# Alternating the products of two Strassen–Winograd multiplications on two PSUM banks each, with sums asked for earlier and half of k-by-v one step later

## The chip, the cores and the metric

The kernel runs on one core of one Trainium2 chip. The metric is the device time of one execution in microseconds (us). Before the change it took 991.92 us in the median of three runs (988.21 to 992.99).

Names in the profile: PE is TensorE's matmul, PEld its weight load, DVE is VectorE, ACT is ScalarE, POOL is GpSimd, SP issues DMAs. "L86" is a line of the kernel; here it is a helper through which every matmul goes (L87 in the changed kernel), as L400 (L405) is for adds, so rows are told apart by the names of their tiles.

## The reference

```python
# q, k, v: 8 batches x 8 heads x 576 x 64, float32;  g_norm: 64
kv  = einsum('bhsd,bhse->bhde', k, v)
out = einsum('bhsd,bhde->bhse', q, kv)
rms = sqrt(mean(out * out, axis=-1, keepdims=True) + 1e-6)
x   = (out / rms * g_norm)            # -> 4608 x 512 (tokens x heads*dim)
h   = x @ w_in                        # 512 -> 2048
g   = maximum(0.01 * h, h)
y   = g @ w_out                       # 2048 -> 512; result 4608 x 512
```

The weights reach the kernel as 64-bit floats and are rounded to 32 bits on the chip, in 32 pieces.

## The kernel before

The 4608 rows are nine blocks of 512. The first block is multiplied in the plain way while weights still arrive and are rounded (`first_block`; tiles `h_ps`, `o_acc`). The other eight use Strassen–Winograd, a scheme that multiplies two matrices, each cut into 2x2 blocks, with seven products of sums of blocks instead of eight, for x·w_in ("h") and for g·w_out ("o"), in four chunks of the hidden width per block. One product is four matmuls of 256 columns (8 entries in the trace, f32). Most products are added to an earlier one in a PSUM bank (a piece of the memory that TensorE writes its results to), and after each of them some engine reads the bank.

```python
BANK = {1: "a", 6: "a", 7: "a", 4: "a", 2: "b", 5: "c", 3: "c"}

def strassen(which, left, right, done):
    banks = {}
    for i in (1, 5, 2, 6, 3, 7, 4):
        first = BANK[i] not in banks
        if first:
            banks[BANK[i]] = ps_m.tile([P, 2, N2], F32, tag=f"{which}{BANK[i]}", ...)
        bank = banks[BANK[i]]
        ...                        # four matmuls into bank
        done(i, bank)              # the reader: an add on VectorE or a copy / leaky relu on ScalarE
        yield

# main loop, per block i and chunk c   (h of chunk c; o of the chunk before)
x_sides = sides_x(xTs.pop(i))      # sums of x, VectorE
...
first = product_h(c, x_sides, g_sides)   # asks for the sums of w_in (GpSimd) itself
go(first, 1)                       # h1
go(second)                         # what is left of the older o
for n in range(5):                 # h5 h2 h6 h3 h7
    go(first, 1)
    if n in (1, 3): go(a_steps, 1) # one step of the attention of a later batch
second = product_o(*before) if before else iter(())
go(second, 1)                      # o1
go(first)                          # h4
for n in range(5):                 # o5 o2 o6 o3 o7
    go(second, 1)
    if n in (1, 3): go(a_steps, 1)
```

The attention steps of a batch, and their places in the first block:

```python
def attention(b):
    ...
    for p in range(NP):            # four pairs of heads
        nc.vector.transpose(qT[:, p, :]..., q_in...)        # 1.25 us on VectorE
        if p % 2 == 0: yield; continue
        attention_kv(b, p // 2, kv_ps)                      # k by v, TensorE, 72 entries
        ...                        # loads of the next two pairs are issued here
        yield
    copy_kv(b, kv_ps); yield       # VectorE
    ...                            # q by kv into o_ps, squares, sums, division

steps.update((i, a1) for a1 in [attention(1)]
             for i in (12, 13, 16, 17, 19, 21, 23, 24, 25, 27, 28))   # first block
```

Rounding one piece of weights takes two ScalarE copies (`add`, `cut`) and four VectorE steps. The 64-bit data lie in one of seven buffers in turn; four of them (`pair0` to `pair3`) later hold GpSimd's sums of weights:

```python
raw_homes = itertools.cycle([(stage, "raw")] * 3 + [(wcomb, f"pair{i}") for i in range(4)])

def round_f64(dst, raw):
    add = spare(...); nc.scalar.activation(add, lo, func=AF.Copy, scale=2.0 ** -29)
    cut = spare(...); nc.scalar.activation(cut, hi..., func=AF.Copy, scale=2.0 ** -112)
    nc.vector.tensor_scalar(cut, cut, ...)               # 1
    nc.vector.tensor_scalar(dst, cut, 3, ...)            # 2
    nc.vector.scalar_tensor_tensor(dst, cut, ..., dst)   # 3
    nc.vector.tensor_tensor(dst, dst, add, op=ALU.add)   # 4
```

## Time and profile before

| | before |
|---|---|
| median of three runs | 991.92 us |
| span of the profiled run | 990.2 us |
| TensorE busy | 958.0 us (97%) |
| TensorE waits from 150 us on | 16.6 us |

At 97% the number that matters is not the busy share but the list of the holes on TensorE. There are two ways to read one. The view of waits gives the idle time with the engine and tile that ended it. The timeline gives more: start to start, an undisturbed product takes 1.73 us here, so whatever exceeds that is lost, whether it was waiting, refilling or a slower clock. The prediction shows both.

For the comparison I cut a span at two points that every variant has: the start of the `o_acc` group just ahead of the attention output of 448 columns in the first block (E, 103.50 us here), and the first Strassen product `h_a` (151.19). The piece between them is F, 47.7 us, the end of the first block; the rest is S, 839.0 us, the eight Strassen blocks.

### The profile page before, as it was taken

What the parts mean: (1) busy time and instruction counts of PE and PEld (TensorE: products, weight loads), DVE (VectorE), ACT (ScalarE), POOL (GpSimd) and SP (SyncE); (2) the same over time, 40 slices, a digit from 0 to 9 for tenths busy, and PEclk for the clock granted to TensorE, in tenths of its full rate; (3) what the DMA queues carried; (4) which work ended last, traced back from release to release, by engine and by line L of the source; (5) the groups of instructions that cost most, each with busy time, mean ns of one, the idle gap of its engine ahead of it and who ended that gap; (6) DMA issues with size and microseconds to landing.
All of it is one profiled execution on the core that took longest, in us unless ns stands there. A gap on an engine that the chain in (4) does not pass through costs nothing.

```text
span 990.2 us, 14098 instructions
## 1 busy us (share of the span) xinstructions
PE 958.0 (97%) x5702; PEld 763.8 (77%) x5702; DVE 435.3 (44%) x688; ACT 268.1 (27%) x531; POOL 499.0 (50%) x395
## 2 busy tenths in 40 slices
PE   8899987999999999999999999999999999999997
PEld 4444435878887888888887888788878888888885
DVE  3968971264234533364335433552245322422223
ACT  3645432331124211421133113311242112112210
POOL 1000214455655665566556666565556666666642
PEclk9899999999999999999999999999999999999999
DMA  9989505300260008000610043003100010001001
GB/s 251 243 214 239 164 1 138 96 1 1 56 178 1 1 2 231 2 1 1 178 56 1 1 121 113 1 1 96 45 1 1 1 43 1 1 1 43 1 1 42
DMA packets 36160, 63.47 MB, mean 64 GB/s; under 512 B 4864, under 2 KB 21248, under 8 KB 36096
## 3 DMA queue, kind: packets, MB, share of 16 engines
q1 hardware_dynamic: 26112, 51.95, 19.9%
q10 hardware_dynamic: 9856, 10.62, 3.2%
q8 instruction: 45, 0.74, 0.3%
q14 instruction: 19, 0.16, 0.1%
q0 software_dynamic: 128, 0.00, 0.0%
HBM read 53.12 MB, written 9.44 MB: 63 GB/s over the span
## 4 chain that ended last, share of the span: by engine, by line
PE 90%; DVE 6%; DMA 2%; ACT 1%; issue 1%; SPq 0%; ACTq 0%; DVEq 0%
PE h_a L86 22%; PE o_a L86 21%; PE h_c L86 11%; PE o_c L86 11%; PE h_b L86 6%; PE o_b L86 6%; PE o_acc L86 5%; PE h_ps L86 5%; PE kv_ps L86 2%; PE o_ps L86 2%; DVE qT L327 1%; DVE sum L289 1%; DMA k_in<-in_k_dram 1%; DMA v_in<-in_v_dram 1%; DMA raw<-in_moe_w_in_dram 1%
## 5 line engine op out<-in xcount | busy, mean ns | idle before, releaser
L400 DVE TENSOR_TENSOR o<-o_a,o 128x512 f32<-128x512 f32 x104 | 71.5, 688 | 122.2 <-PE o_a L86 122.2
L86 PE MATMUL o_a<-wt,gs 128*128 128x256 f32 x512 | 122.1, 381 | 0.0
L400 POOL TENSOR_TENSOR ws<-w 128x512 f32<-128x512 f32 x32 | 44.3, 1385 | 136.6 <-PE h_a L86 97.1
L400 POOL TENSOR_TENSOR wt<-w,w 128x512 f32<-128x512 f32 x32 | 40.9, 1277 | 140.5 <-PE o_a L86 137.4
L86 PEld LDWEIGHTS o_a<-wt,gs 128*128 128x128 f32 x512 | 96.3, 190 | 15.2 <-issue 2.1
L479 ACT ACTIVATE g<-g 128x512 f32<-128x512 f32 x96 | 60.5, 630 | 167.4 <-DVE g L400 167.4
L400 POOL TENSOR_TENSOR gs<-g,g 128x512 f32<-128x512 f32 x64 | 81.3, 1270 | 23.0 <-ACT g L479 22.5
L400 POOL TENSOR_TENSOR ws<-w,w 128x512 f32<-128x512 f32 x32 | 41.9, 1310 | 97.4 <-DMA raw<-in_moe_w_in_dram 94.6
L484 ACT COPY g<-h_a 128x512 f32<-128x512 f32 x32 | 18.7, 585 | 255.5 <-PE h_a L86 244.4
L400 POOL TENSOR_TENSOR wt<-w,wt 128x512 f32<-128x512 f32 x64 | 83.4, 1303 | 2.5
L400 POOL TENSOR_TENSOR wt<-w 128x512 f32<-128x512 f32 x32 | 41.2, 1289 | 65.6 <-PE o_a L86 60.0
L86 PE MATMUL h_a<-xt,w 128*128 128x256 f32 x256 | 62.6, 388 | 7.8 <-DVE g L400 7.8
L86 PE MATMUL h_ps<-xT,w 128*128 128x512 f32 (+1 forms) x136 | 60.5, 589 | 8.1 <-DVE xT L308 4.8
L400 DVE TENSOR_TENSOR g<-h_b,g 128x512 f32<-128x512 f32 x32 | 22.1, 689 | 98.0 <-PE h_b L86 98.0
L400 DVE TENSOR_TENSOR o<-o_c,o 128x512 f32<-128x512 f32 x56 | 38.4, 685 | 57.6 <-PE o_c L86 57.6
L86 PE MATMUL o_a<-wt,g 128*128 128x256 f32 x256 | 60.8, 380 | 1.9 <-DVE o L400 1.9
L86 PE MATMUL h_a<-xT,ws 128*128 128x256 f32 x256 | 62.4, 386 | 0.0
L86 PEld LDWEIGHTS h_a<-xt,w 128*128 128x128 f32 x256 | 48.8, 193 | 17.2 <-DVE g L400 10.6
L86 PE MATMUL h_a<-xT,w 128*128 128x256 f32 x256 | 62.0, 386 | 0.0
L86 PE MATMUL o_a<-w,g 128*128 128x256 f32 x256 | 60.6, 379 | 0.8 <-DVE o L400 0.8
L86 PE MATMUL h_a<-xt,ws 128*128 128x256 f32 x256 | 61.1, 382 | 0.0
L86 PE MATMUL o_c<-wt,gs 128*128 128x256 f32 x256 | 60.8, 381 | 0.0
(86 smaller groups left out, 1741.1 us busy)
## 6 DMA issues: line engine op xcount, KB each, us to landing
out_dram<-o ACTq DMA_DIRECT2D x36, 256.0 KB, 2.2
v_in<-in_v_dram SPq DMA_DIRECT2D x30, 288.0 KB, 5.0
raw<-in_moe_w_in_dram SPq DMA_DIRECT2D x64, 128.0 KB, 5.5
raw<-in_moe_w_out_dram SPq DMA_DIRECT2D x16, 512.0 KB, 6.2
k_in<-in_k_dram SPq DMA_DIRECT2D x28, 288.0 KB, 3.5
q_in<-in_q_dram SPq DMA_DIRECT2D x56, 144.0 KB, 4.5
q_in<-in_q_dram SPq DMA_DIRECT2D x56, 140.0 KB, 4.6
k_in<-in_k_dram ACTq DMA_DIRECT2D x2, 288.0 KB, 9.2
```

Source lines behind the costliest of these rows:

```text
L86: pin(nc.tensor.matmul(*args, **kw))
L289: nc.vector.tensor_add(sums[l], sums[l], sq)
L327: nc.vector.transpose(qT[:, p, :].rearrange("p (t s) -> p s t", s=T), q_in.rearrange("p (s d) -> p s d", d=D)[:, :, :32])
L400: eng.tensor_tensor(out_, a, b_, op=ALU.subtract if minus else ALU.add)
L479: nc.scalar.activation(t, t if src is None else src, func=AF.Prelu, alpha=SLOPE)
L484: nc.scalar.copy(g11, bank)
```

## The change

Its intent: no product should have to wait for the reader of the bank that it writes, and a load should not be waited for. So h and o alternate strictly, the order of the seven products is chosen so that two banks each suffice and alternate too, the second half of k by v comes one step later, and sums are asked for ahead. The core of the diff:

```diff
-        for p in range(NP):
-            ...transpose of pair p...
-            if p % 2 == 0:
+        for m in range(2):
+            turn(2 * m)
+            yield
+            turn(2 * m + 1)
+            if m:
                 yield
-                continue
-            attention_kv(b, p // 2, kv_ps)
+            attention_kv(b, m, kv_ps)
 ...
     def sides_w1(c):                     # sides_w2 likewise
 ...
-        return {1: a11, 2: a12, 3: s4, 4: a22, 5: s1, 6: s2, 7: s3}
+        def more():                      # sums for products 7 and 3, asked for later
+            ...
+        return sides, more
 ...
-    BANK = {1: "a", 6: "a", 7: "a", 4: "a", 2: "b", 5: "c", 3: "c"}
+    ORDER = (1, 2, 6, 5, 7, 3, 4)
+    FRESH = (1, 2, 5)
 ...
+            b = "a" if i in (1, 6, 7, 4) else "c"
 ...
-        accs = [... for t in ("ha", "hb", "oa", "ob")]
+        accs = [... for t in ("oa", "oc", "hb", "ob")]
 ...
-                 for i in (12, 13, 16, 17, 19, 21, 23, 24, 25, 27, 28))
+                 for i in (12, 13, 15, 16, 18, 20, 21, 23, 24, 26, 27, 28))
 ...
+            for t in range(7):
+                go(h_steps, 1)
+                go(o_steps, 1)
+                if t == 3:
+                    h_next, more_h = sides_w1((c + 1) % NC)
+                    o_next, more_o = sides_w2(c)
+                if t == 5:
+                    more_h()
+                if (7 * c + t) % 2:
+                    go(a_steps, 1)
+                if c == NC - 1 and t == 4 and i + 1 < NB:
+                    go(a_steps)
+                    x_sides, more_x = sides_x(xTs.pop(i + 1))
```

## The prediction

> **What bounds the kernel now.** I read the page first: part 1 says who is busy, part 4 who is on the path.
>
> ```profile
> PE 958.0 (97%) x5702; PEld 763.8 (77%) x5702; DVE 435.3 (44%) x688; ACT 268.1 (27%) x531; POOL 499.0 (50%) x395
> ...
> PE 90%; DVE 6%; DMA 2%; ACT 1%; issue 1%; SPq 0%; ACTq 0%; DVEq 0%
> ```
>
> TensorE works for 97% of the span, so a mere change of order can win only the holes between its matmuls and the stretches at a lower clock. The change adds no matmul: the two built kernels have 542 rows each on TensorE, in another order. So I list the holes. The view of waits, TensorE only, from 150 us on (the Strassen part):
>
> ```profile
> PE h_a L86 <- DVE g L400: 7.8, 7, 2.1
> PE kv_ps L86 <- DMA v_in<-in_v_dram: 6.1, 2, 5.1
> PE o_a L86 <- DVE o L400: 2.7, 4, 0.9
> ```
>
> The waits sum to 16.6 us. They cost more than that, so I price them from start to start. In the timeline of TensorE an undisturbed product (4 matmuls of 256 columns, 8 entries) starts 1.73 us after the one before. Around the worst hole:
>
> ```profile
> 161.13 2.00 PE L86 MATMUL h_a<-xT,ws 128*128 128x256 f32 x8
> 163.90 1.99 PE L86 MATMUL h_a<-xt,w 128*128 128x256 f32 x8 [0.78 <-DVE g L400]
> 166.96 0.29 PE L86 MATMUL kv_ps<-v_in,k_in 64*64 64x64 f32 x2 [1.06 <-DMA v_in<-in_v_dram]
> 172.31 2.19 PE L86 MATMUL kv_ps<-v_in,k_in 64*64 64x64 f32 x70 [5.06 <-DMA v_in<-in_v_dram]
> 174.43 3.45 PE L86 MATMUL h_a<-xT,w 128*128 128x256 f32 x8
> 177.72 1.89 PE L86 MATMUL h_c<-xt,ws 128*128 128x256 f32 x8
> ```
>
> From 163.90 to 177.72 lie 13.82 us for two products and one k-by-v group (1.21 us start to start elsewhere): 1.73+1.73+1.21 = 4.67. **Loss 9.15 us**, of which 6.1 is waiting; the rest is the slow clock after it (3.29 us for the product at 174.43). The next kind, again TensorE alone:
>
> ```profile
> 425.09 1.89 PE L86 MATMUL o_a<-w,g 128*128 128x256 f32 x8
> 427.93 1.99 PE L86 MATMUL h_a<-xt,w 128*128 128x256 f32 x8 [0.95 <-DVE g L400]
> ```
>
> 2.84 instead of 1.73. Two products of h into bank a stand with one product between; the reader of the bank, an add on VectorE, stood behind attention work. This happens at 321, 425, 530, 634 and 738 us (1.1 each; with two small ones, 0.45 in sum: 6.1). Its bad case is at 217.91 (wait 2.12, then 3.15 and 2.10 us for two products): 4.1. The tail has three more, where bank a follows bank a directly: 967.07 to 969.84 to 972.59, and 981.32 to 984.09, 1.04 each: 3.1. **Sum of holes after 163 us: 9.15+6.1+4.1+3.1 = 22.4 us.**
>
> **What the Trainium skill says.** "TensorE: Matmul & The Clock Gate", The HAM clock gate: after an idle window of about 3.4 us the array runs at half clock until it has been busy again for as long. The trace agrees in the factor (3.29 against 1.73) but a wait of 2.12 us was already enough at 217.91, while waits of 1.5 us and less left the clock alone. "SBUF — State Buffer", Who interferes with whom: VectorE and GpSimd share one port pair, an exclusive lock; two-input adds and 2-port modes on VectorE block against a reading GpSimd. The trace agrees: the rounding of weights, VectorE, with GpSimd idle (first three rows) and with GpSimd adding from 138.98 to 143.56 (last three):
>
> ```profile
> 137.15 0.43 DVE L197 TENSOR_SCALAR w<-cut 128x512 uint32<-128x512 uint32 x1
> 137.61 0.69 DVE L198 SCALAR_TENSOR_TENSOR w<-cut,w 128x512 uint32<-128x512 uint32 x1
> 138.33 0.69 DVE L200 CUSTOM_DVE_ANT_0 w<-w,add 128x1024 uint16<-128x1024 uint16 x1
> ...
> 139.40 1.37 DVE L197 TENSOR_SCALAR w<-cut 128x512 uint32<-128x512 uint32 x1
> 140.80 1.63 DVE L198 SCALAR_TENSOR_TENSOR w<-cut,w 128x512 uint32<-128x512 uint32 x1
> 142.47 1.64 DVE L200 CUSTOM_DVE_ANT_0 w<-w,add 128x1024 uint16<-128x1024 uint16 x1
> ```
>
> "PSUM — Partial Sum Buffer", PSUM bank collisions: the bank must be guarded as a whole. That is why a product waits for its bank's reader even if it accumulates.
>
> **The change part by part.**
>
> 1. *Interleave, two banks each.* The built order is h1 o1 h2 o2 h6 o6 h5 o5 h7 o7 h3 o3 h4 o4, banks a c a c a c a for each of h and o (o1 is of the chunk before). Between two uses of a bank there are now three products (5.2 us), except that h4 and the next h1, and o4 and the next o1, have one. A reader starts some 0.2 us after its product's next has started and takes 0.6 (ScalarE) to 0.69 us (VectorE), so with one product between it has 0.75 us to spare, with three over 4. The h4 reader is a ScalarE activation now, and on VectorE the order near o4 has no attention instruction next to it. I went through the heaviest stretch (last chunk of a block: two qT transposes of 1.26, sums, the division): the tightest add there has about 1.5 us left. So the five 1.1 us waits and the 4.1 us event go: **-10.2 us**. In the first chunk, which has no o to put between, h4 to h1 is adjacent, about 1.0 us; it replaces the 1.04 at 161.13. Net 0.
> 2. *Second k-by-v group later.* In the built order it stands nine products after the first, not one. Its loads are issued when the first group ends (161.2 us) and the last landed at 172.3: 11.1 us, against 9 x 1.73 = 15.6 us of room. The wait and its slow clock go: **-9.15 us**.
> 3. *Tail.* The last o alternates a and c; only o4 to o1 is adjacent. Two of three waits go: **-2.1 us**.
> 4. *Sums moved.* GpSimd has 12 adds of 1.27 us per chunk of 14 products: 15.2 of 24.2 us, as before. Sums of weights come half a chunk ahead, since each pair buffer is refilled as soon as its second product is read. In the last chunk it makes four sums of weights that nobody uses (401 rows against 397), 5 us beside the matmuls. Sums of x: same adds, two steps ahead. **0 us.**
> 5. *End of the first block.* Here the order of two engines changes. Now TensorE loses 1.3 and 1.7 us:
>
> ```profile
> 134.34 3.60 PE L86 MATMUL o_acc<-w,gT 128*128 128x512 f32 x8
> 139.08 3.70 PE L86 MATMUL h_ps<-xT,w 128*128 128x512 f32 x8 [1.15 <-DVE w L200]
> 144.25 7.11 PE L86 MATMUL o_acc<-w,gT 128*128 128x512 f32 x16 [1.47 <-DVE w L200]
> ```
>
> Two of the three last weight pieces are rounded earlier in the new order, so these 3.0 us go. But the very last piece (the weights of the last o_acc group) now stands on ScalarE behind the activation of the last h_ps, and the same event lets GpSimd start its sums. Counting from 134.34: the last h_ps ends at 134.34+2x3.43 = 141.2; activation and two ScalarE copies about 1.9, so 143.1; four VectorE steps at the blocked durations 0.42+1.37+1.63+1.64 with gaps 5.2, so 148.4. The last o_acc could have started at 141.2+3.43 = 144.7. New wait 3.7, and after so long a wait I expect the half clock, some 2 us more (1.8 at 217.91, 3.0 at 172). **-3.0+5.7 = +2.7 us.**
>
> Sum: 990.2-10.2-9.15-2.1+2.7 = 971.5 us of span; the timed run is 1.7 longer than its span (991.89 against 990.2): 973.2. I add 0.8 for small new waits (a 512-wide attention output on ScalarE just ahead of an h4 reader, an issue of a store behind an add): **974.0 us**, 1.8% less.
>
> **The rivals.**
>
> *A: VectorE becomes the bound between products.* For: 44% busy in bursts, and its reads of o are now interleaved with h. Against: 3 products between uses of a bank, and 10 adds of 0.69 are only 6.9 of 24.2 us per chunk. If the one-product places (two per chunk, 62 in all) each lost 0.3 us, +19 us: about 990, nothing won.
>
> *B: GpSimd.* Its sums of g, w and the weights stand in one queue. For: 63% load in the Strassen part and refills that wait for a product to be read. Against: from the end of h3 the six sums and two refills take about 9 us, and the first user, o6, comes 8 products (13.8 us) after h3. If wrong, each chunk could lose some us: 1000 and more.
>
> *C: the loads were the only gain.* If the small waits come back elsewhere, only part 2 and the tail are won: 990.2-11.2+2.7+1.7 = 983.
>
> *D: the end of the first block goes well* (last piece rounded without the block, or the clock kept): 2 to 4 us less: 970 to 972, just over 2%.
>
> **Range and chances.** The holes bound the gain: 22.4 us after 163 and 3.0 in the first block, so nothing under 966 is possible, and 2% means under 972.1 (against the median 991.92; the three runs before spread over 4.8 us). My sum ends 2 us above that line, with part 5 (2.7) the least sure; what I overlooked is likelier a new wait than a new gain. Range 969 to 982; faster by over 2%: 0.25, within 2%: 0.73, slower: 0.02.
>
> **What would show it.** TensorE's waits after 150 us should fall from 16.6 to about 2 to 4 us, with no DMA wait on kv_ps; the waits on "g" for h_a gone or turned into one on ScalarE's activation in the first chunk. In the tail one wait instead of three. About 148 us a wait of 3 to 4 us of o_acc for a rounded weight, followed by a product or two at half clock; if it is missing, part 5 is wrong and the time is near 970. Per-product pitch stays at 1.73. Many waits of h_a on ScalarE or o_a on VectorE at the seams of chunks would make A right; waits on ws, wt or gs of GpSimd, B.

## The result

| | before | after |
|---|---|---|
| median, same chip, 4 runs each | 992.45 us (988.21 to 993.62) | 977.11 us (976.25 to 978.28) |
| span of the profiled run | 990.2 us | 974.5 us |
| E / F / S | 103.5 / 47.7 / 839.0 | 103.4 / 54.1 / 817.0 |

The ratio is 0.9854, with a 95% interval of 0.9827 to 0.9881: 1.5% less time, inside the 2% band. Ratios are the mean time of one kernel's runs over that of the other's runs of the same rounds, so they are not quite the ratio of the medians quoted.

From the page of the kernel after, part 1 and the engines' shares of the chain that ended last (the prediction shows these for the kernel before):

```profile
PE 954.6 (98%) x5702; PEld 762.3 (78%) x5702; DVE 430.2 (44%) x688; ACT 270.1 (28%) x531; POOL 507.9 (52%) x399
...
PE 94%; DVE 2%; DMA 2%; ACT 1%; issue 0%; SPq 0%; ACTq 0%
```

The matmuls are as many as before. VectorE's share of the chain fell from 6% to 2%. The waits of TensorE from 150 us on, after (total us, times, longest):

```profile
PE o_acc L87 <- DVE w L201: 3.7, 1, 3.7
PE o_a L87 <- DVE o L405: 0.8, 1, 0.8
PE h_a L87 <- ACT g L484: 0.7, 1, 0.7
```

That is 5.2 us instead of 16.6, and of these 3.7 belong to the first block. The wait for `v_in` is gone. Busy time in the stretch from 160 to 200 us; columns: stretch, its length, PE, PEld, DVE, ACT, POOL busy with counts, granted clock, DMA share, GB/s. First before:

```profile
160.00:200.00 40.00, 33.10 (x294) 26.92 (x295) 11.02 (x18) 11.75 (x23) 21.22 (x17) 0.91 0.47 118
```

Then after:

```profile
160.00:200.00 40.00, 39.31 (x325) 33.15 (x324) 9.13 (x13) 11.68 (x22) 22.36 (x18) 1.00 0.46 119
```

TensorE is busy for 39.3 of 40 us instead of 33.1, and the granted clock is 1.00 instead of 0.91: both the wait for the load and the slow clock behind it are gone. From 200 to 900 us it is busy all the time, in every hundred.

So the Strassen part gained 22.0 us, and the end of the first block gave 6.4 back. Where? The timeline of TensorE in the first block, before:

```profile
103.50 3.60 PE L86 MATMUL o_acc<-w,gT 128*128 128x512 f32 x8
107.02 0.98 PE L86 MATMUL o_ps<-qT,kv 64*32 64x448 f32 x16
107.94 3.70 PE L86 MATMUL h_ps<-xT,w 128*128 128x512 f32 x8
```

And after:

```profile
103.44 3.60 PE L87 MATMUL o_acc<-w,gT 128*128 128x512 f32 x8
108.62 1.16 PE L87 MATMUL o_ps<-qT,kv 64*32 64x448 f32 x12 [1.58 <-DVE kv L260]
...
110.84 3.70 PE L87 MATMUL h_ps<-xT,w 128*128 128x512 f32 x8
```

From the first row to the last it is 4.44 us before and 7.40 after: 2.96 us lost. The copy of kv comes at 108.30 on VectorE instead of 103.73. k by v itself, at 95.26 instead of 91.89, had long ended by then, and both kernels round 25 weight pieces ahead of the copy. What is new is a wait of VectorE for a ScalarE copy (`cut`), whose queue now holds an activation ahead of it. ScalarE and then VectorE, after:

```profile
95.37 0.60 ACT L565 ACTIVATE gT<-h_ps 128x512 f32<-128x512 f32 x1 [5.16 <-PE h_ps L87]
```

```profile
97.13 0.43 DVE L195 TENSOR_SCALAR cut<-cut 128x512 f32<-128x512 f32 x1 [4.55 <-ACT cut L194]
```

In the kernel before, the ScalarE copies of five pieces ran from 89.05 to 94.92 us with no activation between them, and VectorE shows no idle time from 90.31 until the copy of kv. Now only the first of these pieces comes ahead of the activation, which waits for `h_ps` until 95.37. VectorE's 4.55 us of idle time match the 4.57 by which the copy is late. The end of the block, after:

```profile
151.36 6.32 PE L87 MATMUL o_acc<-w,gT 128*128 128x512 f32 x8 [3.65 <-DVE w L201]
157.51 1.89 PE L87 MATMUL h_a<-xT,w 128*128 128x256 f32 x8
```

The last `o_acc` group waits 3.65 us for the last rounded weight piece, and then takes 6.15 us start to start instead of 3.51 (the same group at full clock, in the run "GpSimd's sums wait for the last piece" below): 2.64 us for the half clock. The granted clock is 0.50 from 149.9 to 156.7 us (view of windows in steps of 0.2 us). VectorE's last three rounding steps, which it waits for, after:

```profile
146.50 1.37 DVE L198 TENSOR_SCALAR w<-cut 128x512 uint32<-128x512 uint32 x1
147.91 1.63 DVE L199 SCALAR_TENSOR_TENSOR w<-cut,w 128x512 uint32<-128x512 uint32 x1
149.57 1.64 DVE L201 CUSTOM_DVE_ANT_0 w<-w,add 128x1024 uint16<-128x1024 uint16 x1
```

And GpSimd at the same time, in the same run:

```profile
146.09 1.51 POOL L405 TENSOR_TENSOR ws<-w 128x512 f32<-128x512 f32 x1 [26.80 <-ACT cut L194]
```

GpSimd had idled for 26.8 us and was released by the same ScalarE copy (`cut`) as VectorE, because the raw data of that last piece lay in the buffer (`pair0`) that its sums fill.

### The profile page after: what moved, and what is told of

It reads as the page before. It is cut to its first block, busy times and chain, and to the rows that moved or that the text cites. A ratio compares the mean times of both kernels' runs of the same rounds, so it can differ in the third digit from the quotient of the medians.

```text
span 974.5 us, 14053 instructions
## 1 busy us (share of the span) xinstructions
PE 954.6 (98%) x5702; PEld 762.3 (78%) x5702; DVE 430.2 (44%) x688; ACT 270.1 (28%) x531; POOL 507.9 (52%) x399
## 4 chain that ended last, share of the span: by engine, by line
PE 94%; DVE 2%; DMA 2%; ACT 1%; issue 0%; SPq 0%; ACTq 0%
PE h_a L87 23%; PE o_a L87 23%; PE h_c L87 17%; PE o_c L87 17%; PE h_ps L87 5%; PE o_acc L87 5%; PE o_ps L87 2%; DMA k_in<-in_k_dram 2%; PE kv_ps L87 2%; DMA raw<-in_moe_w_in_dram 1%; DVE w L199 0%; DVE w L201 0%; ACT cut L194 0%; DVE qT L329 0%; DVE xT L309 0%
## 5 line engine op out<-in xcount | busy, mean ns | idle before, releaser
L405 POOL TENSOR_TENSOR ws<-w 128x512 f32<-128x512 f32 x33 | 46.4, 1407 | 288.6 <-PE h_c L87 247.7
L405 DVE TENSOR_TENSOR o<-o_c,o 128x512 f32<-128x512 f32 x88 | 60.5, 687 | 89.5 <-PE o_c L87 89.5
L405 DVE TENSOR_TENSOR g<-h_c,g 128x512 f32<-128x512 f32 x64 | 44.0, 688 | 85.6 <-PE h_c L87 85.6
L87 PE MATMUL o_acc<-w,gT 128*128 128x512 f32 x128 | 60.7, 619 | 3.7 <-DVE w L201 3.7
L87 PE MATMUL h_c<-xT,w 128*128 128x256 f32 x256 | 61.1, 381 | 0.0
L87 PE MATMUL h_c<-xt,ws 128*128 128x256 f32 x256 | 61.1, 381 | 0.0
L87 PE MATMUL h_c<-xT,ws 128*128 128x256 f32 x256 | 60.5, 379 | 0.0
```

Of the source, the lines that this page charges most:

```text
L87: pin(nc.tensor.matmul(*args, **kw))
L405: eng.tensor_tensor(out_, a, b_, op=ALU.subtract if minus else ALU.add)
```

## The experiments

Ten kernels ran, three rounds each; a ratio is to the runs of the kernel before on the same chip (medians 992.45 to 993.37). All outputs are right. E, F and S are those of each profiled run. Against the line of 2% only the last two of the table are faster; the first block in the old order is unclear, since its interval holds 0.98.

| run | median us | ratio to before (95%) | E | F | S |
|---|---|---|---|---|---|
| before | 992.45 | 1 | 103.5 | 47.7 | 839.0 |
| after | 977.11 | 0.9854 (0.9827, 0.9881) | 103.4 | 54.1 | 817.0 |
| k by v later alone | 981.47 | 0.9881 (0.9866, 0.9895) | 105.5 | 47.7 | 826.6 |
| all but k by v later | 982.50 | 0.9892 (0.9877, 0.9906) | 104.8 | 53.1 | 821.2 |
| three banks, old order | 979.97 | 0.9866 (0.9849, 0.9884) | 105.6 | 54.5 | 819.3 |
| sums not ahead | 977.38 | 0.9841 (0.9824, 0.9858) | 104.5 | 54.3 | 817.2 |
| two reads more at o4 | 996.06 | 1.0035 (1.0018, 1.0053) | 104.5 | 53.1 | 835.9 |
| two reads more at o2 | 977.65 | 0.9845 (0.9830, 0.9859) | 104.2 | 54.3 | 817.7 |
| last piece elsewhere | 977.99 | 0.9849 (0.9834, 0.9863) | 104.0 | 55.8 | 816.7 |
| first block in the old order | 973.34 | 0.9804 (0.9787, 0.9820) | 106.2 | 47.7 | 817.1 |
| sums wait for the last piece | 971.90 | 0.9784 (0.9768, 0.9799) | 104.9 | 48.6 | 817.0 |
| both of the last two | 969.85 | 0.9765 (0.9751, 0.9780) | 105.6 | 46.0 | 817.0 |

The theory after the result: the alternation wins what bank readers cost, the distance between the halves of k by v wins the load wait, and the first block gives 6.4 us back for two reasons: kv's copy is late (2.96), because ScalarE's copies for the rounding are, and VectorE and GpSimd block each other at the last piece (3.4 net of what the reorder won). The rivals: the later k by v is the whole gain; the number of banks or VectorE's load is what matters; the losses in the first block have another cause.

### k by v later alone

The kernel before with the new attention steps for batches 2 and on, nothing else.

```diff
-        a_steps = attention(i + 1) if i + 1 < B else iter(())
+        a_steps = attention_new(i + 1) if i + 1 < B else iter(())   # second half one step later
```

> The kernel before, with nothing changed but the second k-by-v group one step later in batches 2 to 7. In the built order five products stand between the two groups in block 1 instead of two. Theory (the wait at 167 to 172 us is the time of the loads, 11.1 us after the first group): 5 x 1.73 + 1.0 of room leave a wait of about 1.5 us and no half clock, so 7 to 8 us less than before, about 984.5 us; the 1.1 us waits of h_a on VectorE's adds at five places and the tail's three waits stay. Rival (the loads come later by as much as the group is moved): no gain, 992.

Measured: 981.47 us, 3 us better than expected. No wait for the load is left (I had expected 1.5 us), and S fell by 12.4 us, more than the 9.15 of the load wait. The excess is the bad event at 217.91 us (4.1 us in the prediction): with the attention steps shifted by one, the wait there is 0.59 us and the clock stays up. The small VectorE waits did not go; they changed their tile. TensorE's waits for VectorE's add into o in this run:

```profile
PE o_a L86 <- DVE o L427: 6.6, 9, 0.9
```

Before there were seven waits on g (7.8 us) and four on o (2.7); now there is one on g and nine on o. The add that happens to stand behind attention instructions on VectorE makes its bank late: at 425 us in the kernel before the add into g (427.21, after two transposes), in this run the one into o (425.74, after two transposes).

### All but k by v later

The changed kernel with the old attention steps for batches 2 and on.

```diff
-        a_steps = attention(i + 1) if i + 1 < B else iter(())
+        a_steps = attention_old(i + 1) if i + 1 < B else iter(())   # second half as before
```

> The changed kernel with the second k-by-v group at its old step in batches 2 to 7 (the first block as in the changed kernel). In the built order five products (8.7 us, with 0.7 of wait 9.4) stand between the groups of batch 2, eight (13.8 us) in later batches, against loads of about 11 us. Theory (the interleave alone has already moved the groups apart): one wait of 1.5 to 2 us for v in block 1, with at most 2 us of half clock after it, none later: 979 to 981 us. Rival (the later group is what removed the 9.15 us): a wait of 5 us as before, 985 or more.

Measured: 982.50 us, outside what I had expected. And the expected wait for v is not there. TensorE in this run:

```profile
175.90 1.28 PE L87 MATMUL kv_ps<-v_in,k_in 64*64 64x64 f32 x72
...
228.82 1.99 PE L87 MATMUL o_a<-w,g 128*128 128x256 f32 x8 [1.46 <-DVE o L428]
```

The second half of k by v starts at 175.90 us, 11.0 us after the first half (164.90), without a wait: the new loop spaces the attention steps two turns apart, and that is enough for the load. What this run lost is at 228.82 and, with waits of 0.95 and 0.30 us, at two other seams: o1 waits for the add of o4, which at 228 us stood on VectorE behind two transposes of 1.25 us, sums and the start of the division. So the later k by v is worth 4.2 us inside the new loop (S 821.2 against 817.0), not through the load: 3.2 us are these three seams, start to start (1.61, 1.11 and 0.46), and so VectorE's queue; the other 1.0 us was not traced. The two parts overlap: alone they win 12.4 and 17.8 us, together 22.0.

### Three banks in the old order, still alternating

```diff
-    ORDER = (1, 2, 6, 5, 7, 3, 4)
+    ORDER = (1, 5, 2, 6, 3, 7, 4)
+    BANK = {1: "a", 6: "a", 7: "a", 4: "a", 2: "b", 5: "c", 3: "c"}
 ...
-            b = "a" if i in (1, 6, 7, 4) else "c"
+            b = BANK[i]
 # and GpSimd's first three sums of g after product 7 instead of 3
```

> The changed kernel with its strict alternation of h and o, but with the old order of products (1 5 2 6 3 7 4) and three banks each instead of two. It tells what the new order with two banks does by itself. In the alternation, bank a follows bank a with one product between at 7 to 4 and at 4 to the next 1, for h and for o: four one-product places per chunk instead of two. My theory: one product between leaves 0.75 us to spare, enough for a reader that starts at once, so the alternation carries nearly all of the gain: 976 to 980, with a few waits of 0.1 to 1 us where VectorE is busy at 7 to 4. Rival: the new order with two banks is what matters; then half of the 10 us come back: 982 to 988, waits of h_a and o_a of 5 us or more in sum.

Measured: 979.97 us, S 819.3: 19.7 of the 22.0 us without the two-bank order. No wait appeared between 180 and 950 us. The rest is where h or o has no partner to alternate with; the tail of this run:

```profile
961.72 1.99 PE L87 MATMUL o_a<-w,g 128*128 128x256 f32 x8 [0.79 <-DVE o L405]
...
973.22 1.97 PE L87 MATMUL o_a<-wt,g 128*128 128x256 f32 x8 [0.87 <-DVE o L405]
```

The second of these, and one like it in the first chunk (0.78), are not in the changed kernel. So the alternation carries the gain, and the new order is worth the 2.3 us at both ends (it also leaves two banks unused in the Strassen part).

### Sums not ahead

The sums are asked for when their chunk begins, as before the change.

```diff
-                if t == 3:
-                    h_next, more_h = sides_w1((c + 1) % NC)
-                    o_next, more_o = sides_w2(c)
-                if t == 5:
-                    more_h()
 # instead: all four sums of w_in ahead of product_h, all four of w_out ahead of product_o
```

> The changed kernel with the sums of weights asked for when their chunk begins, as the kernel before did, instead of half a chunk ahead; everything else stays. My theory: the scheduler already puts each sum as soon as its buffer is free, and the built order differs from the changed kernel's only by the four sums nobody uses (GpSimd 397 rows instead of 401). So 976 to 978, profile span 974 to 975, TensorE's waits after 150 us still 5.2. Rival: asking for the sums ahead is what keeps TensorE from waiting for them; then waits on ws and wt of GpSimd appear, some tenths per chunk, and the time is 982 or more.

Measured: 977.38 us, S 817.2, the same waits. That part of the change does nothing here: the scheduler had already put each sum where its buffer comes free.

### Two more reads at one place and at another

Two copies of the bank to a scratch tile on VectorE, after o4 (one product before the bank is written again) or after o2 (three products).

```diff
             done(i, bank)
+            if which == "o" and i == 4:            # the other run: i == 2
+                for _ in range(2):
+                    scratch = work.tile([P, 2, N2], F32, tag="scratch", name="scratch")
+                    nc.vector.tensor_copy(scratch, bank)
             yield
```

> The changed kernel with two more VectorE reads (copies of 128x512, about 0.69 us each, to a scratch tile) of the bank after product o4, where only one product lies between this bank's reader and the next writer. My theory (a seam with one product between has 0.75 us to spare): in three chunks of four the reader is a VectorE add of 0.69, the two copies end 0.5 to 0.6 us too late; in the first chunk of a block the first reader is ScalarE and the copies run beside it, so they are just in time. 24 places x 0.6 = 14 us: 988 to 994, and the waits of o_a on VectorE's scratch sum to 10 to 18 us. Rival (VectorE's total load matters, not the place: 32 x 2 x 0.69 = 44 us more of it): the same time as the next run, whatever it is.

> As the run before, but the same two more reads follow product o2, where three products lie between this bank's reader and its next writer (over 4 us to spare, 1.4 used). The load of VectorE is the same as in the run before. My theory: 976.5 to 978.5, waits after 150 us 5 to 7 us. Rival (load, not place): the same time as the run before.

Measured: 996.06 and 977.65 us, with 42 and 38 us more on VectorE. The waits of TensorE for these reads after o4:

```profile
PE o_a L87 <- DVE scratch L476: 13.6, 25, 2.2
```

And after o2:

```profile
PE o_c L87 <- DVE scratch L476: 0.5, 1, 0.5
```

The place decides, not VectorE's load. One of the seams after o4, on TensorE:

```profile
329.45 1.89 PE L87 MATMUL h_a<-xT,w 128*128 128x256 f32 x8
331.81 1.97 PE L87 MATMUL o_a<-w,g 128*128 128x256 f32 x8 [0.47 <-DVE scratch L476]
```

It is 2.36 us start to start, 0.63 over 1.73. VectorE's add ends at 330.34 us and the two copies at 331.67, 1.33 us later; 1.33 - 0.63 = 0.70 us to spare, close to the 0.75 of the prediction. The total came out above my 988 to 994, since a listed wait costs more than its idle time: 0.63 here and 0.08 more in the product after it, 0.71 for a wait of 0.47. 24 x 0.71 = 17.0, and 1.4 more at the start of the tail, give 18.4 of the 18.9 us by which S grew.

### The last piece's raw data elsewhere

```diff
+    raw_homes = itertools.chain(itertools.islice(raw_homes, 31), itertools.repeat((stage, "raw")))
```

> The changed kernel, but the raw data of the very last weight piece lies in a staging buffer instead of the buffer that the first sums of weights use, so GpSimd's sums are no longer released by the same event as the last four rounding steps on VectorE. Theory (lock of the shared port, then half clock): the last steps take 0.43+0.43+0.69+0.69 instead of 0.43+1.37+1.63+1.64, so the wait of the last o_acc falls from 3.65 to about 0.8 us, and the slow group after it (6.15 us start to start instead of 3.43) is gone: 5.5 us less, about 971.6 us. Rival (the position of the piece on ScalarE behind the last activation is the cost, not the lock): the wait stays near 3 us and the time near 977. What can spoil it: the sums move to 100 to 115 us, where VectorE is busy, and may lengthen the wait for the copy of kv (1.58) by 1 to 2 us; then about 973.

Measured: 977.99 us, nothing won, F 55.8 instead of 54.1. The last `o_acc` wait did fall, to 0.83 us, without a half clock. But `pair0` was now free 45 us earlier, so GpSimd's sums ran at 101 to 112 us, beside other rounding steps, which slowed to 1.37 to 1.64 us and pushed the copy of kv back to 113.72. The wait that the prediction had missed grew instead, on TensorE in this run:

```profile
114.05 3.05 PE L87 MATMUL o_ps<-qT,kv 64*32 64x448 f32 x16 [6.43 <-DVE kv L261]
```

A miss in time, but telling: the blocking moves with GpSimd's sums. It needed a run that lets them start neither early nor at the same time.

### The first block in the old order

The changed kernel with the old steps and the old attention for batch 1.

```diff
-    steps.update((i, a1) for a1 in [attention(1)]
-                 for i in (12, 13, 15, 16, 18, 20, 21, 23, 24, 26, 27, 28))
+    steps.update((i, a1) for a1 in [attention_old(1)]
+                 for i in (12, 13, 16, 17, 19, 21, 23, 24, 25, 27, 28))
```

> The changed kernel with the order of attention steps of the kernel before in the first block alone (k by v of batch 1 one step earlier, old list of positions); the Strassen part is that of the changed kernel. Theory (the first block costs 6.3 us: the first product of h starts at 157.51 instead of 151.19): it starts at 151 again, with the waits of 1.15 and 1.47 for rounded weights back, and the time is about 970.8 us, over 2% less than before. Rival (those 6.3 us are chance of the run, or are given back later in the Strassen part): the time stays at 976 to 978.

Measured: 973.34 us; F is 47.7 as before the change, S 817.1. So the whole 6.4 us of F come from the reorder of the first block. Both waits of before for rounded weights are back (1.14 and 1.48 us), and VectorE's idle 4.55 us ahead of the copy of kv is gone. But the time is 2.5 us over what I had expected: by the medians only 3.8 us came back, since E is longer (106.2). TensorE in E, in this run:

```profile
94.63 1.27 PE L87 MATMUL kv_ps<-v_in,k_in 64*64 64x64 f32 x70 [1.34 <-DMA v_in<-in_v_dram]
```

In the old order the second half of k by v of batch 1 comes one `h_ps` group earlier and can catch its load still under way: the four profiled runs with that order waited 0, 0.95, 1.34 and 0.29 us there, the eight with the new order not at all. From start to start it costs 1.65 us here; the rest by which E is longer than after, 1.1 us, lies before 90 us and was not traced. So the reorder of the first block can also win something in E, and its net price is under 6.4 us in such runs.

### GpSimd's sums wait for the last piece

The temporary that the very last rounding step reads (`rounds` counts the pieces) lies in `pair0`, so the sums can't start before that step has ended. The order on TensorE, VectorE, ScalarE and GpSimd is exactly that of the changed kernel.

```diff
+    raw_homes = itertools.chain(itertools.islice(raw_homes, 31), itertools.repeat((stage, "raw")))
 ...
-        add = spare(a * n, "add", U32)
+        if next(rounds) == 31:
+            add = wcomb.tile([P, a * n], U32, tag="pair0", name="add")
+        else:
+            add = spare(a * n, "add", U32)
```

> The changed kernel with one dependence more: the temporary that the very last rounding step reads lies in the buffer which GpSimd's first chunk sums fill (its raw data goes elsewhere), so these sums can't start before the last VectorE step is done. The order on every engine is the same as in the changed kernel. My theory (the two engines block each other there): the last four rounding steps take 0.43, 0.43, 0.69, 0.69 instead of 0.43, 1.37, 1.63, 1.64, the last o_acc waits 0.8 instead of 3.65 us, no half clock follows (2.6 us), GpSimd's sums start about 3 us later and are still in time for h6: 977.1 - 2.8 - 2.6 = 971.7, span 969. The earlier kv copy wait of 1.6 us in the first block stays, unlike in the run in which the sums came free too early. Rival (the last wait is set by something else, such as the load of the last piece or ScalarE): the steps or the wait keep their length and the time stays at 977; or the sums are now late and h6 waits for ws by 2 us or more: 974 to 976.

Measured: 971.90 us. The last two rounding steps, VectorE:

```profile
148.45 0.69 DVE L205 SCALAR_TENSOR_TENSOR w<-cut,w 128x512 uint32<-128x512 uint32 x1
149.18 0.69 DVE L207 CUSTOM_DVE_ANT_0 w<-w,add 128x1024 uint16<-128x1024 uint16 x1
```

GpSimd's first sum, and TensorE's last `o_acc` group, in the same run:

```profile
150.02 1.26 POOL L411 TENSOR_TENSOR ws<-w 128x512 f32<-128x512 f32 x1 [29.24 <-DVE w L207]
```

```profile
150.02 3.67 PE L87 MATMUL o_acc<-w,gT 128*128 128x512 f32 x8 [0.83 <-DVE w L207]
```

The same steps in the same order take 0.69 us instead of 1.63 and 1.64 once GpSimd no longer adds beside them; the wait is 0.83 instead of 3.65, the group runs at full clock, and F is 5.4 us shorter, as worked out ahead (2.8 + 2.6). This shows the cause of that part. The kv wait of 1.6 us stays.

### Both

> The changed kernel with the first block's old order of attention steps (measured 973.3 by itself) and the added dependence of the run before in this list. In that earlier run GpSimd's sums blocked the rounding of the last but one piece: steps of 1.37, 1.64, 1.64 instead of 0.43, 0.69, 0.69 (2.9 us more), and the waits were 1.14 and 1.48. My theory: without the block the second wait (1.48) goes, the first (1.14, VectorE behind the division) stays: 971.8, span 969.5. If the two remedies add up in full, it is the best version, 2.1% below the kernel before. Rival: the first wait grows by what the second loses, since another engine sets it: 973.3, no gain.

The edit is the sum of the last two. Measured: 969.85 us, 2.35% less than before by the ratio: the fastest version. TensorE at the end of its first block:

```profile
141.21 3.70 PE L87 MATMUL h_ps<-xT,w 128*128 128x512 f32 x8 [1.14 <-DVE w L207]
144.75 7.03 PE L87 MATMUL o_acc<-w,gT 128*128 128x512 f32 x16
```

The second wait (1.47 before the change) is gone, the first is left; F is 46.0, 1.7 us less than before the change. It is 2 us better than I had expected; 0.6 us of that is a shorter E than in the run with the old order alone, the rest was not traced.

## Why the prediction was right, point by point

The class (within 2%) and the range (969 to 982) held; the figure of 974.0 was 3.1 us too low. By spans it was 2.2 us too low (972.3 against 974.5); the other 0.9 us is that the profiled run was the fastest of its four.

- **Holes after 163 us (part 1 and part 3).** Right in size: with part 2 they were to be 21.45 us, and S fell by 22.0. The slack of 0.75 us at a one-product place, on which the answer to rival A rested, was measured as 0.70 in the run with two more reads at o4, and the tail has one wait instead of three. That a product waits for its bank's reader even if it accumulates, which the prediction put down to a rule about banks, needs no such rule here: the reader reads the same columns that the product adds to. No run separates the two reasons.
- **k by v later (part 2).** Right in size, incomplete in cause. "The wait and its slow clock go" was put down to the later step. The run without that step had no load wait either: either of the two edits moves the halves far enough apart, and inside the new loop the later step pays by 4.2 us, 3.2 of them through VectorE's queue.
- **Sums (part 4).** 0 us, as the control showed.
- **End of the first block (part 5).** The mechanism was right: the wait was 3.65 us (predicted 3.7), the steps lasted 1.37, 1.63 and 1.64 as predicted, and the run in which GpSimd waits shows the cause. It ended at 151.36 us rather than about 148, so the waits after 150 us sum to 5.2 us and not to "about 2 to 4"; without it they are 1.5. The half clock was under-sized: 2.64 us instead of "some 2 us more". That makes +3.4 instead of +2.7. Its size is partly chance: in other runs with the same order and the same wait it cost 1.7 to 3.0 us.
- **What was missing.** The failed step is the list of new waits in the first block, which had only its end. The copy of kv behind the rounding steps cost 2.96 us more. I had read there which weight pieces come earlier, and not which ones the new order puts behind an activation on ScalarE: VectorE idles 4.55 us for them. It is the first half of part 5's mechanism (a piece behind the activation of an `h_ps`) a second time, earlier in the block. The sum with it: -22.0 + 2.96 + 3.4 = -15.6, and 990.2 - 974.5 = 15.7.
- **The 0.8 us allowance** was for small new waits in the Strassen part; none came. It covered part of what was missing in the first block.
- **Rivals.** A (VectorE between products) and B (GpSimd) did not happen: no wait from 180 to 950 us. C (only the load and the tail, 11.2 us) is refuted by S, which fell by 22.0, and by all but k by v later, which lost neither the load's gain nor more than 4.2 us of the rest. D (the end goes well) did not happen by itself, but the run that makes it happen reaches 971.9, just over the 2%.

Open: why E scatters by up to 2.8 us between profiled runs, beyond the waits of k by v for its load (up to 1.34 us). Whether the half clock at the last group would return under a wait between 0.83 and 3.65 us was not tried.

## What to carry to other kernels

When TensorE is nearly full, list its holes from start to start and ask of each bank how many products lie between its reader and its next writer: one left about 0.7 us, three left room for two more reads at no cost. A reorder that empties one stretch should be checked for what it pushes back on the other engines' queues elsewhere, here ScalarE's copies, and with them the copy of kv and the last weight piece; the engine that waits (VectorE) need not be the one whose order did it. And if two engines slow each other on a critical piece of work, a dependence that delays the one that is in no hurry can be worth more than freeing its buffer early.

## What the Trainium skill lacked or had wrong

- "TensorE: Matmul & The Clock Gate", The HAM clock gate, names an idle window of about 3.4 us before the half clock. In the kernel before, a wait of 2.12 us was already followed by a product of 3.15 us instead of 1.73; waits of up to 1.62 us after 90 us left it alone, and so did one of 2.20 us in the tail of the run with two more reads at o4 (from it to the end 16.5 us, as after its 0.79 us in the changed kernel). Where a wait falls in the window decides too. In the granted clock the stretches at half clock last 3.41, 6.83 or 10.24 us, and within a run they begin on one grid of 3.41 us (kernel before: 170.60 and 218.38 us, 14 steps apart). The step that ended at 218.38 held the whole wait of 2.12 us; the wait of 2.20 us lay across a line of its run's grid, at 976.15, with 1.23 and 0.97 us on the two sides. So a step with 2.12 us idle was enough, and steps with up to 1.62 us idle were not.
- The same section says that the window runs free, and calls the cost at a kernel's start variable; for a wait within a kernel it gives no such spread. Here the same `o_acc` group after the same wait of 3.65 to 3.66 us lost 2.64 us (after), 1.7 (all but k by v later) and 3.0 (three banks). It is half of the time that the group spent at half clock: from its start at 151.4, 153.9 (where the half clock began) and 153.5 us to the clock's return at 156.7, 157.3 and 159.6.
- "SBUF — State Buffer", Who interferes with whom, is right on who blocks whom, but gives no duration for such steps: beside GpSimd's f32 adds of 128x512 the last three went from 0.43, 0.69 and 0.69 us to 1.37, 1.63 and 1.64, and with GpSimd held back they returned to 0.43, 0.69 and 0.69 in the same order of instructions.
- I found on none of the pages that I used how much more a wait for a bank costs than its listed idle time: 0.47 us listed cost 0.71 from start to start with the product after it. Of the difference, 0.16 is that an undisturbed product is listed at 1.89 us and repeats every 1.73.
